# A spectral block and two MLPs on one core: bias written by ScalarE, another mixing unit in three float32r passes, two-bank tiles in the inverse transform

## The chip, the cores and the metric

The kernel runs on one core of one Trainium2 chip. The time is device microseconds of one execution; the median of the runs counts. Five engines work side by side: TensorE (PE: matmuls, and PEld: its weight loads), VectorE (DVE), ScalarE (ACT), GpSimd (POOL) and SyncE (SP). SyncE and GpSimd issue the transfers; an accumulating transfer (GpSimd's queue) adds its source to what lies at its destination.

## What is computed

Batch 2, 3008 positions, 256 channels. A real Fourier transform along the positions, a complex 256 x 256 mixing with a bias, a soft threshold on the real and the imaginary part, the inverse transform, then two MLPs (256 to 2048 to 256) over all 6016 tokens:

```python
X = np.fft.rfft(x, axis=1)
Yr = Xr @ w_r - Xi @ w_i + b_r
Yi = Xr @ w_i + Xi @ w_r + b_i
Yr = np.sign(Yr) * np.maximum(np.abs(Yr) - lam, 0.0)
...
y = np.fft.irfft(Y, n=x.shape[1], axis=1)
...
h = x @ w_in
g = h * (1.0 / (1.0 + np.exp(-1.702 * h)))
return (g @ w_out).astype(np.float32)
```

The second MLP has exp(-h) in place of exp(-1.702 h). Inputs and outputs are float32.

## The kernel before

**Stages.** Everything is unrolled, and within each engine the instructions keep the order in which the program writes them (`region(...)`, with a manual schedule). The stages are: the forward transform (16 groups, loop over `groups`), the mixing (12 units, loop over `mids`), the inverse (16 steps: q, b, t), and the MLPs (2 layers x 6 blocks of tokens x 8 parts, `group`). The forward and inverse transforms are matmuls against cosine and sine matrices, folded by symmetry.

**A mixing unit** (`mid_mm`) makes two groups of sums, each in one PSUM bank of 512 columns: a group is four matmuls of 512 columns. Units 0 and 1 (`n32` = 2) run them in float32, which the trace shows as two records per matmul. The later ones split both operands into a high and a low float32r part and make three passes (high x high, high x low, low x high). The first group also takes a matmul of ones against `bias_hl` (L572), whose row 0 is the high part of the bias, and row 1 the low part.

**Splitting.** `xsplit(i, 0)` makes the high part xh of unit i (a ScalarE copy, L500), `xsplit(i, 1)` the low part xl: ScalarE writes -x (L496), and a transfer on GpSimd's queue adds x (L497), so that the rounding is left. In the loop, iteration i makes xl of unit i + 3 and xh of unit i + 2; the first split unit's xl is made in forward group 10. The matrix's parts, wh (ScalarE, L550) and wl (VectorE, L551), are made at the stage's start.

**After a unit's matmuls**, one iteration later: ScalarE copies the first bank to SBUF (`us`, L578), VectorE makes sum and difference (`sd`, L580 to L582), ScalarE a relu (L588) and VectorE the threshold (L593); another iteration later VectorE folds (L605) into the inverse's operands. The threshold's two halves are separate instructions of 512 columns.

**Weight conversion beside it.** The MLP weights come as 64-bit floats and are converted on the way: load on SyncE (`raw`, L162 to L166), a ScalarE step (`cv_c`, L180), five VectorE steps (L185 to L189), and a transfer on GpSimd's queue that adds the rest (`cv_a`, L190). One is in work at a time. `tf` names the forward groups, `tm` the mixing units, `ti` the inverse steps in which one starts. The loads of the inverse's matrices (`load_m`, SyncE) stand in the units of `li` and the steps of `lii`.

**The inverse.** Two PSUM pools of four banks, ps0 and ps1. Steps with t = 0, 1 write two banks of ps0, steps with t = 2, 3 two banks of ps1 (`inv_mm`). One step later VectorE takes the banks out (`inv_post`): for t = 0, 1 into `rt`, after a ScalarE copy of one bank (`eo`, L697); for t = 2, 3 as `ac = rt + psi` and `rt = rt - psi` (L716, L717), bank by bank. `inv_out` writes the tokens into `yt`: two quarters by VectorE (L747), two by ScalarE (L749) and accumulating transfers (L751). `ac` is one SBUF tile, except for (q, b) = (1, 0). The last step's two halves are made inside the first MLP group. Step 8 of 16 is the ninth.

**The MLP** groups are matmuls without a gap in three passes each (L846, L874).

Of the kernel before, what the change touches and what calls it, by code (L numbers as in the profile page):

```python
# [9 lines left out]
F32 = mybir.dt.float32  # L10
CFG = {'lv0': 'V', 'lv': 'V', 'dd0': 'VPVVPPPPPVVP', 'dd': 'V', 'ths': 'VVVVPV', 'thf': 'V', 'ivf': 'V', 'cva': 'P', 'pol': 'PPPP', 'pil': 'P', 'mvl': 'PVVP', 'xl': 'V', 'xse': 'V', 'gl': 'VPPPPPPP', 'tf': [6, 10, 13], 'tm': [0, 2, 4, 6, 8, 10], 'ml': [], 'pk': 6, 'ti': [3], 'pi': 4, 'pl': [1, 4, 8, 10, 13], 'kb': [0, 1, 1, 1, 1, 1, 1, 0], 'kr': [0, 1, 0, 1, 0, 1, 1, 0], 'fa': 3, 'xp': [2, 4, 4, 5], 'xq': [1, 4, 1], 'xs': 4, 'xi': [7, 7, 9, 10, 10, 11, 8], 'xsi': 9, 'xo': (0, 1, 6, 2, 3, 4, 5), 'xd': (0, 1, 4, 6), 'ca': 4, 'tl': True, 'fwd': 'all', 'rest0': 'all', 'rest1': 'all', 'last1': 'all', 'inv': 'all', 'mid': 'all', 'last0': 'all', 'thm': 'A', 'gl0': 'PVPVVVPV', 'gl2': 'PPPPPPPP', 'gl3': 'PPPPPPPV', 'xl0': 'VVVVVPV', 'xl1': 'V', 'pre': 13, 'pre2': 0, 'yd': 6, 'lvb': 6, 'mlp': 'all', 'pr': 'V', 'pf': 'V', 'eo': '0111', 'n32': 2, 'li': [3, 5, 7], 'lii': [0], 'xa': 4, 'nhb': 6, 'ddb': 6, 'mlp1': 'all', 'mlp2': 'all'}
NUM = dict(li=[5, 6, 7, 8], n32=2, pk=4, ydp=2, lii=[1, 3], xd=(), ml=[], pl=[], xo=range(7), pi=6, nhb=6, tf=[5, 9, 13], tm=[1, 3, 5, 7, 9, 11], ti=[0, 2, 4, 6, 8, 10, 12, 14, 14, 15, 15], kb=[2] * 8, kr=1, fa=3, fe=2, pm=0, nf=4, lvb=6, ddb=8, ivb=1, eob=1, fsb=6, f1=3, f2=0, fm=[7, 8, 9], fi=[1, 1, 2, 2], pre=13, pre2=1, yd=3, psh=0, ie=[12], xp=[1, 3, 4, 5], xq=[1, 2, 2], xs=5, nw=4, xi=[14, 14, 15, 15], xsi=13, rw=2, ca=4, cc=2, tb=1, tmn=1)
# [9 lines left out]
P = 128  # L22
# [34 lines left out]
def spectral_mlp_kernel(ctx, tc, xin, mfwd, minv, wc, bias, w_in1, w_out1, w_in2, w_out2, outT):  # L57
# [4 lines left out]
    def N(k):  # L62
        return CFG.get(k, NUM[k])

# [486 lines left out]
    nc.vector.tensor_sub(wl, wc_s, r32(wh))  # L551

    def mid_mm(i):
        b, p, j = mids[i]
        x = [xt[b, p, j, cs][:, q] for cs in range(2) for q in range(2)]
        hl = [[xsp[b, p, j, cs, k][:, q] for k in range(2)] for cs in range(2) for q in range(2)] if i >= N('n32') else None
        ps = []
        for grp in range(2):
            t = bank(i, "psm")
            n = 0  # L560

            for xi, off in ((0, 0), (3, D)) if grp == 0 else ((1, 0), (2, D)):
                for mm in range(2):
                    w = slice(off, off + 2 * D)
                    if hl is None:
                        nc.tensor.matmul(t, x[xi][:, mm], wc_s[:, mm, w], start=(n == 0), stop=(n == 3 and grp == 1))  # L566
# [18 lines left out]
    def mid_relu(i, sd):  # L585
        th = mid_p.tile([P, 2, 512], F32, tag="th", name="th")
        for h in range(2):
            nc.scalar.activation(th[:, h], sd[:, h], AF.Relu, bias=neglam)  # L588
        return i, sd, th

    def mid_th(i, sd, th):
        for h in range(2):
            nc.vector.scalar_tensor_tensor(out=th[:, h], in0=sd[:, h], scalar=LAM, in1=th[:, h], op0=ALU.add, op1=ALU.min)  # L593
        return i, th

    def mid_fold(i, th):
        b, p, j = mids[i]
        for q in range(2):
# [14 lines left out]
            elif pairs:  # L613
                ft[q, b, p, -1] = ft.pop((q, b, p, 0))

    post = thr = None
# [31 lines left out]

    region('inv')
    modes[0] = True  # L650

# [4 lines left out]
    def inv_mm(q, b, t, mms=range(2), out=None):  # L656
# [21 lines left out]
    RW = 2 * 378  # L678

    def row(x, mm, t, n):  # L680
        if isinstance(x, dict):
            return x[t, mm][:, :n]
        return x[:, t * RW + mm * 378 : t * RW + mm * 378 + n]

    def inv_post(q, b, t, ps, mms=range(2)):
# [37 lines left out]
    def inv_out():  # L723
        q, b, ac, rt = ydone.pop(0)
        todo, col = [], b * S + (0 if q == 0 else HALF)
        for k in range(4):
            x = ac if k < 2 else rt
            if isinstance(x, dict):
                todo.extend((k, yt[:, mm, col : col + 376], x[0, mm][:, :376], x[1, mm][:, :376]) for mm in range(2))
                col += 376  # L730
                continue
            u, v = (x[:, t * RW : (t + 1) * RW].rearrange("p (m c) -> p m c", m=2) for t in range(2))
            if q == 0 and k == 1:
# [128 lines left out]
    def group(l, i, p, hook):  # L862
# [71 lines left out]
        if begun:  # L934
            out_next()
        else:
            inv_post(*prev[:3], inv_mm(*prev[:3], (1,), ps), (1,))
            inv_out()
        hook(5)
        prod(X, 2, 5, False)  # L940
# [236 lines left out]
```

## Time and profile before

| | |
|---|---|
| runs shown, median (lowest to highest) | 1147.75 us (1147.16 to 1149.87) |
| the profiled execution's own time | 1147.49 us |
| its span in the trace | 1145.7 us |
| TensorE busy | 1138.4 us (99%) |
| ScalarE, VectorE, GpSimd busy | 775.3, 609.0, 469.9 us |
| mixing stage | from 59.01 to 130.05 us |
| inverse, to the first matmul of the MLP | from 130.05 to 172.26 us |

The page gives the busy time of each engine, the costliest groups of instructions, and the chain of work that ended last. The stretch view gives busy time between two moments. The chain in order of time gives, for each piece, its start, its length and its engine, tile and line. The time views of one engine give start, length, line, form, and in brackets the idle time before it and what ended it. A record of a matmul is longer than its distance to the next, since matmuls overlap; lengths of the chain are distances.

### The profile page before, as it was taken

Reading aid. Unit: us, or ns where it says so; the run is one execution under the profiler, and the core shown is the slowest. Engines: PE = TensorE matmul, PEld = TensorE weight load, DVE = VectorE, ACT = ScalarE, POOL = GpSimd, SP = SyncE. Lnnn points to the kernel's source line nnn. Section 1 sums busy time; section 2 is a strip of 40 time slices with the busy share of each in tenths; the row PEclk is TensorE's granted clock in tenths of the full one; section 3 lists DMA queues with packets and bytes.
Section 4 is the critical chain, followed back from the end, with each engine's and each line's share of the span. In section 5 each row is a group of like instructions: output and inputs, shape, how many; then the busy total and the mean of one; then the engine's idle time right before and its main releaser. Section 6 shows DMA issues by size and latency. Waiting matters only on the chain.

```text
span 1145.7 us, 14644 instructions
## 1 busy us (share of the span) xinstructions
PE 1138.4 (99%) x5094; PEld 946.4 (83%) x5094; DVE 609.0 (53%) x1015; ACT 775.3 (68%) x1445; POOL 469.9 (41%) x410
## 2 busy tenths in 40 slices
PE   9999999999999999999999999999999999999998
PEld 6868987888888888888889878888888888888897
DVE  7888997764565465564554533523523523523422
ACT  2587357877677676686677876766765866756665
POOL 0253164444444434444446646443334433344333
PEclk9999999999999999999999999999999999999999
DMA  8699494431221212112211000010000100100100
GB/s 328 155 183 242 116 160 87 103 72 37 59 52 37 74 37 63 49 38 74 56 37 37 28 28 19 1 38 1 29 10 1 37 1 1 37 1 1 37 1 33
DMA packets 39852, 68.69 MB, mean 60 GB/s; under 512 B 3681, under 2 KB 16225, under 8 KB 39778
## 3 DMA queue, kind: packets, MB, share of 16 engines
q1 hardware_dynamic: 26306, 45.51, 12.2%
q0 software_dynamic: 13472, 22.24, 11.4%
q8 instruction: 40, 0.66, 0.2%
q14 instruction: 34, 0.28, 0.1%
HBM read 35.15 MB, written 10.35 MB: 40 GB/s over the span
## 4 chain that ended last, share of the span: by engine, by line
PE 95%; ACT 2%; DVE 2%; issue 1%; DMA 1%; SPq 0%; POOL 0%; DVEq 0%; POOLq 0%; ACTq 0%
PE o L846 43%; PE x L874 38%; PE psm L569 5%; PE psi L387 4%; PE psf L387 3%; PE psm L566 1%; ACT yt L877 1%; DMA xr<-in_x 1%; DVE keep L313 0%; SPq L477 0%; ACT g L879 0%; ACT yt L893 0%; PE psm L572 0%; ACT x L781 0%; DVE x L788 0%
## 5 line engine op out<-in xcount | busy, mean ns | idle before, releaser
L884 POOL TENSOR_TENSOR g<-yt,g 128x512 fp32r<-128x512 f32 (+1 forms) x282 | 357.6, 1282 | 502.8 <-PE x L874 316.7
L846 PE MATMUL o<-g,wo 128*128 128x512 f32 (+1 forms) x2304 | 559.8, 385 | 0.0
L846 PEld LDWEIGHTS o<-g,wo 128*128 128x128 f32 x2304 | 432.5, 188 | 80.8
L874 PE MATMUL x<-x,wi 128*128 128x512 f32 (+1 forms) x2016 | 498.5, 386 | 0.5
L874 PEld LDWEIGHTS x<-x,wi 128*128 128x128 f32 x2016 | 377.5, 188 | 75.1 <-ACT yt L893 1.7
L877 ACT ACTIVATE yt<-yt 128x512 f32<-128x512 f32 (+1 forms) x288 | 179.5, 623 | 263.6 <-DVE yt L924 216.6
L879 ACT CAST g<-yt 128x512 fp32r<-128x512 f32 (+1 forms) x384 | 236.0, 615 | 12.1
L924 DVE TENSOR_TENSOR yt<-yt,x 128x512 f32<-128x512 f32 (+1 forms) x96 | 64.8, 675 | 216.8 <-PE x L874 216.5
L896 DVE TENSOR_TENSOR yt<-yt,x 128x512 f32<-128x512 f32 (+1 forms) x96 | 64.9, 676 | 182.4 <-ACT yt L893 181.3
L884 DVE TENSOR_TENSOR g<-yt,g 128x512 fp32r<-128x512 f32 (+1 forms) x102 | 70.1, 687 | 65.9 <-ACT g L879 65.9
L190 POOL DMA_DIRECT2D cv_a<-cv_c x32 | 28.4, 889 | 111.4 <-DVE cv_c L189 105.0
L929 DVE TENSOR_TENSOR yt<-yt,x 128x512 f32<-128x512 f32 (+1 forms) x96 | 64.8, 675 | 0.3 <-issue 0.3
L788 DVE TENSOR_TENSOR x<-yt,x 128x512 fp32r<-128x512 f32 (+1 forms) x55 | 43.1, 783 | 36.1 <-ACT x L781 36.1
L877 ACT ACTIVATE yt<-x 128x512 f32<-128x512 f32 (+1 forms) x96 | 56.1, 584 | 0.0
L914 ACT COPY yt<-x 128x512 f32<-128x512 f32 (+1 forms) x96 | 55.8, 581 | 0.1
L912 ACT COPY yt<-x 128x512 f32<-128x512 f32 (+1 forms) x96 | 54.9, 572 | 1.4 <-PE x L874 1.4
L893 ACT COPY yt<-x 128x512 f32<-128x512 f32 (+1 forms) x96 | 54.9, 572 | 0.0
L387 PE MATMUL psi<-m,f 128*128 128x188 f32 (+3 forms) x224 | 45.2, 357 | 0.0
L387 PEld LDWEIGHTS psi<-m,f 128*128 128x128 f32 x224 | 37.6, 190 | 5.5
L387 PE MATMUL psf<-m,xf 128*128 128x190 f32 (+2 forms) x176 | 36.1, 366 | 0.6 <-DVE xf L332 0.6
L781 ACT CAST x<-yt 128x512 fp32r<-128x512 f32 (+1 forms) x59 | 36.5, 618 | 0.0
L387 PEld LDWEIGHTS psf<-m,xf 128*128 128x128 f32 x176 | 29.6, 190 | 7.3 <-DVE xf L332 0.9
(123 smaller groups left out, 803.9 us busy)
## 6 DMA issues: line engine op xcount, KB each, us to landing
raw<-in_wi SPq DMA_DIRECT2D x32, 256.0 KB, 3.6
cv_a<-cv_c POOLq DMA_DIRECT2D x32, 256.0 KB, 5.2
raw<-in_wo SPq DMA_DIRECT2D x16, 512.0 KB, 3.9
xl<-xt POOLq DMA_DIRECT2D x20, 256.0 KB, 8.4
out_t<-yt SPq DMA_DIRECT2D x20, 256.0 KB, 2.1
raw<-in_x SPq DMA_DIRECT2D x9, 512.0 KB, 6.3
wi<-tmp POOLq DMA_DIRECT2D x8, 256.0 KB, 4.8
w_in<-cv_a SPq DMA_DIRECT2D x8, 256.0 KB, 2.0
```

The lines of the kernel that those rows point to most:

```text
L387: nc.tensor.matmul(ps, hi[:, c : c + P], m[:, k, :w], start=i == 0, stop=i == last)
L569: nc.tensor.matmul(t, st, mv, start=n == 0 and k == 0, stop=n == 3 and grp == 1 and k == 2)
L846: nc.tensor.matmul(acc[h, mm], st, mv, start=first and k == 0, stop=last and k == 2)
L874: nc.tensor.matmul(ps, st, mv, start=first and m == 0, stop=m == 2, skip_group_check=True)
L877: nc.scalar.activation(g, g if src is None else src, func)
L879: nc.scalar.copy(gh, g)
L884: eng.tensor_sub(gl, g, r32(gh))
L893: nc.scalar.copy(y1, X)
L896: nc.vector.tensor_add(y1, y1, Y)
L914: nc.scalar.copy(y3, X)
L924: nc.vector.tensor_add(y2, y2, X)
L929: nc.vector.tensor_add(y3, y3, Z)
```

## The change

It does six things.

- The bias of units 4 to 11 is no longer a matmul: ScalarE copies it into the bank of the first group ahead of the unit (`put_bias(i + 1)` in iteration i, behind `mid_sd`), and the unit's matmuls add to what is there. The host gives the bias spread over 128 rows; it is loaded into `bias_f` in forward group 9.
- Unit 1 is split too (`n32` 2 to 1). Its xl is made in forward group 10; its xh and unit 2's xl at the stage's start.
- `tm` goes from [0, 2, 4, 6, 8, 10] to [1, 3, 5, 7, 9, 11].
- `li` goes from [3, 5, 7] to [6, 8, 9].
- Relu and threshold become one instruction of 1024 columns each.
- In the inverse ps1 is opened anew with two tiles of two banks, and steps with t = 2, 3 have both halves in one of them; VectorE takes both with one sum and one difference (the last step, inside the MLP, keeps its halves). `ac` of (0, 1) and (1, 0) lies in a part of `yt` that is written later. In the first MLP group ps1 is opened again with four banks.

```diff
-        nc.sync.dma_start(out=bias_f[0:1], in_=bias)
+        nc.sync.dma_start(out=bias_f[0:1], in_=bias[0:1])
...
+        if g == 9:
+            nc.sync.dma_start(out=bias_f, in_=bias)
         if g == 10:
-            xsplit(N('n32'), 1)
+            xsplit(1, 1)
...
+    xsplit(1, 0)
+    xsplit(2, 1)
...
-            t = bank(i, "psm")
+            ready = i in filled and grp == 0
+            t = filled.pop(i) if ready else bank(i, "psm")
...
-                            nc.tensor.matmul(t, st, mv, start=n == 0 and k == 0, stop=n == 3 and grp == 1 and k == 2)
+                            nc.tensor.matmul(t, st, mv, start=n == 0 and k == 0 and not ready, stop=n == 3 and k == 2 and (ready or grp == 1), skip_group_check=ready)
...
-            if grp == 0:
+            if grp == 0 and not ready:
                 nc.tensor.matmul(t, ones, bias_hl, start=False, stop=True)
...
-        for h in range(2):
-            nc.scalar.activation(th[:, h], sd[:, h], AF.Relu, bias=neglam)
+        nc.scalar.activation(th, sd, AF.Relu, bias=neglam)
...
-        for h in range(2):
-            nc.vector.scalar_tensor_tensor(out=th[:, h], in0=sd[:, h], scalar=LAM, in1=th[:, h], op0=ALU.add, op1=ALU.min)
+        nc.vector.scalar_tensor_tensor(out=th, in0=sd, scalar=LAM, in1=th, op0=ALU.add, op1=ALU.min)
...
+    def put_bias(i):
+        if 4 <= i < len(mids):
+            filled[i] = bank(i, "psm")
+            nc.scalar.copy(filled[i], bias_f)
...
         sd = mid_sd(*post) if post is not None else None
+        put_bias(i + 1)
         xsplit(i + 3, 1)
         xsplit(i + 2, 0)
...
+    closed("ps1")
+    ps_p[1] = opened("ps1", bufs=2, space=PS)
...
-        out = out or [bank(t // 2, "psi") for _ in range(2)]
+        if out is None and p:
+            d = ps_p[1].tile([P, 1024], F32, tag="pd", name="psi")
+            out = [d[:, :512], d[:, 512:], d]
+        out = out or [bank(0, "psi") for _ in range(2)]
...
-            if (q, b) == (1, 0):
-                ac[0] = {(h, mm): slot(1, F32, "ac") for h in range(2) for mm in range(2)}
+            if q != b:
+                ac[0] = [yt[:, :, c : c + 378 - 2 * q] for c in ((NT - 752, NT - 376) if q else (NT - 1504, NT - 1126))]
...
-        for mm in mms:
+        if len(mms) == 2:
+            r, a, d = both(rt[0], t - 2, n), both(ac[0], t - 2, n), ps[2].rearrange("p (m c) -> p m c", m=2)[:, :, :n]
+            nc.vector.tensor_add(a, r, d)
+            nc.vector.tensor_sub(r, r, d)
+        for mm in mms if len(mms) == 1 else ():
```

`both` gives the two halves of a tile as one operand. `mid_mm` in float32 (unit 0 alone now) is as it was.

## Rows read from the trace of the kernel before

**Rows 1.** The page, part 1: span; busy us (share) and instructions by engine.
```profile
span 1145.7 us, 14644 instructions
...
PE 1138.4 (99%) x5094; PEld 946.4 (83%) x5094; DVE 609.0 (53%) x1015; ACT 775.3 (68%) x1445; POOL 469.9 (41%) x410
```

**Rows 2.** Stretch view, TensorE: stretch, length, busy (instructions), clock, DMA share.
```profile
23.40:1142.20 1118.80, 1117.48 (x5018) 1.00 0.22 54
```

**Rows 3.** Chain by time: start us, length us, engine, tile, line, instructions.
```profile
59.01 3.43 PE psm L566 x8
...
62.67 6.87 PE psm L566 x16
...
87.57 5.45 PE psm L569 x24
93.02 0.23 PE psm L572
...
104.61 5.45 PE psm L569 x24
...
127.33 2.72 PE psm L569 x12
```

**Rows 4.** ScalarE by time, later in mixing: start, length, line [idle before].
```profile
101.53 0.57 ACT L578 COPY us<-psm 128x512 f32<-128x512 f32 x1
...
120.14 0.68 ACT L180 ACTIVATE cv_c<-raw 128x512 f32<-128x512 f32 x1 [2.01 <-DMA cv_a<-cv_c]
```

**Rows 5.** ScalarE by time, start of the mixing stage.
```profile
55.42 0.68 ACT L180 ACTIVATE cv_c<-raw 128x512 f32<-128x512 f32 x1 [3.54 <-DMA raw<-in_wi]
...
60.47 1.48 ACT L550 CAST wh<-wc_s 128x1536 fp32r<-128x1536 f32 x1
...
62.89 1.13 ACT L500 CAST xh<-xt 128x512 fp32r<-128x512 f32 x2
...
70.10 1.34 ACT L588 ACTIVATE th<-sd,neglam 128x512 f32<-128x512 f32 x2
```

**Rows 6.** VectorE by time, start of the mixing stage.
```profile
61.98 1.76 DVE L551 TENSOR_TENSOR wl<-wc_s,wh 128x1536 fp32r<-128x1536 f32 x1
```

**Rows 7.** Tile view of xl, its last line.
```profile
DMA to landing us min/median/max: 3.5/8.4/10.8
```

**Rows 8.** DMA issues, 60 to 66 us: queue, KB each, median landing us.
```profile
xl<-xt POOLq DMA_DIRECT2D x2, 256.0 KB, 3.9
```

**Rows 9.** DMA issues, 40 to 135 us.
```profile
xl<-xt POOLq DMA_DIRECT2D x20, 256.0 KB, 8.4
...
m<-in_mi SPq DMA_DIRECT2D x2, 384.0 KB, 9.7
...
m<-in_mf SPq DMA_DIRECT2D x1, 376.0 KB, 3.6
bias_hl<-bias_f POOLq DMA_DIRECT2D x1, 2.0 KB, 2.7
```

**Rows 10.** POOL's queue by time, end of the forward stage.
```profile
43.62 0.54 POOL L367 DMA_DIRECT2D bias_hl<-bias_f  x1 [4.71 <-DVE bias_f L366]
```

**Rows 11.** SyncE's queue by time, end of the forward stage.
```profile
49.03 0.38 SPq L162 DMA_DIRECT2D raw<-in_wi  x1
```

**Rows 12.** VectorE by time, end of the mixing stage and inverse.
```profile
121.67 0.43 DVE L185 TENSOR_SCALAR cv_c<-cv_c 128x512 f32<-128x512 f32 x1
...
123.79 0.69 DVE L189 SCALAR_TENSOR_TENSOR cv_c<-raw,cv_c 128x512 f32<-128x512 uint32 x1
...
130.16 0.69 DVE L580 TENSOR_TENSOR sd<-us,psm 128x512 f32<-128x512 f32 x1 [0.81 <-PE psm L569]
...
149.26 0.55 DVE L429 TENSOR_TENSOR rt<-psi,eo 128x376 f32<-128x376 f32 x1
```

**Rows 13.** Stretch view of psi, inverse to its ninth step.
```profile
130.05:150.70 20.65, 20.65 (x129) 20.65 (x129) 7.40 (x14) 1.91 (x4) 1.00 0.45 94
```

**Rows 14.** Tile view of yt, 150 to 165 us: min/median/max ns, forms.
```profile
L747 DVE TENSOR_TENSOR yt<-rt x3: 544/549/947, 156.9 to 158.2; 128x752 f32<-128x752 f32 x1, 128x376 f32<-128x376 f32 x1, 128x374 f32<-128x374 f32 x1
```

More of the change, by code (lines that the diff above doesn't have):

```diff
@@ L10 @@
 F32 = mybir.dt.float32
-CFG = {'lv0': 'V', 'lv': 'V', 'dd0': 'VPVVPPPPPVVP', 'dd': 'V', 'ths': 'VVVVPV', 'thf': 'V', 'ivf': 'V', 'cva': 'P', 'pol': 'PPPP', 'pil': 'P', 'mvl': 'PVVP', 'xl': 'V', 'xse': 'V', 'gl': 'VPPPPPPP', 'tf': [6, 10, 13], 'tm': [0, 2, 4, 6, 8, 10], 'ml': [], 'pk': 6, 'ti': [3], 'pi': 4, 'pl': [1, 4, 8, 10, 13], 'kb': [0, 1, 1, 1, 1, 1, 1, 0], 'kr': [0, 1, 0, 1, 0, 1, 1, 0], 'fa': 3, 'xp': [2, 4, 4, 5], 'xq': [1, 4, 1], 'xs': 4, 'xi': [7, 7, 9, 10, 10, 11, 8], 'xsi': 9, 'xo': (0, 1, 6, 2, 3, 4, 5), 'xd': (0, 1, 4, 6), 'ca': 4, 'tl': True, 'fwd': 'all', 'rest0': 'all', 'rest1': 'all', 'last1': 'all', 'inv': 'all', 'mid': 'all', 'last0': 'all', 'thm': 'A', 'gl0': 'PVPVVVPV', 'gl2': 'PPPPPPPP', 'gl3': 'PPPPPPPV', 'xl0': 'VVVVVPV', 'xl1': 'V', 'pre': 13, 'pre2': 0, 'yd': 6, 'lvb': 6, 'mlp': 'all', 'pr': 'V', 'pf': 'V', 'eo': '0111', 'n32': 2, 'li': [3, 5, 7], 'lii': [0], 'xa': 4, 'nhb': 6, 'ddb': 6, 'mlp1': 'all', 'mlp2': 'all'}
+CFG = {'lv0': 'V', 'lv': 'V', 'dd0': 'VPVVPPPPPVVP', 'dd': 'V', 'ths': 'VVVVPV', 'thf': 'V', 'ivf': 'V', 'cva': 'P', 'pol': 'PPPP', 'pil': 'P', 'mvl': 'PVVP', 'xl': 'V', 'xse': 'V', 'gl': 'VPPPPPPP', 'tf': [6, 10, 13], 'tm': [1, 3, 5, 7, 9, 11], 'ml': [], 'pk': 6, 'ti': [3], 'pi': 4, 'pl': [1, 4, 8, 10, 13], 'kb': [0, 1, 1, 1, 1, 1, 1, 0], 'kr': [0, 1, 0, 1, 0, 1, 1, 0], 'fa': 3, 'xp': [2, 4, 4, 5], 'xq': [1, 4, 1], 'xs': 4, 'xi': [7, 7, 9, 10, 10, 11, 8], 'xsi': 9, 'xo': (0, 1, 6, 2, 3, 4, 5), 'xd': (0, 1, 4, 6), 'ca': 4, 'tl': True, 'fwd': 'all', 'rest0': 'all', 'rest1': 'all', 'last1': 'all', 'inv': 'all', 'mid': 'all', 'last0': 'all', 'thm': 'A', 'gl0': 'PVPVVVPV', 'gl2': 'PPPPPPPP', 'gl3': 'PPPPPPPV', 'xl0': 'VVVVVPV', 'xl1': 'V', 'pre': 13, 'pre2': 0, 'yd': 6, 'lvb': 6, 'mlp': 'all', 'pr': 'V', 'pf': 'V', 'eo': '0111', 'n32': 1, 'li': [6, 8, 9], 'lii': [0], 'xa': 4, 'nhb': 6, 'ddb': 6, 'mlp1': 'all', 'mlp2': 'all'}
 NUM = dict(li=[5, 6, 7, 8], n32=2, pk=4, ydp=2, lii=[1, 3], xd=(), ml=[], pl=[], xo=range(7), pi=6, nhb=6, tf=[5, 9, 13], tm=[1, 3, 5, 7, 9, 11], ti=[0, 2, 4, 6, 8, 10, 12, 14, 14, 15, 15], kb=[2] * 8, kr=1, fa=3, fe=2, pm=0, nf=4, lvb=6, ddb=8, ivb=1, eob=1, fsb=6, f1=3, f2=0, fm=[7, 8, 9], fi=[1, 1, 2, 2], pre=13, pre2=1, yd=3, psh=0, ie=[12], xp=[1, 3, 4, 5], xq=[1, 2, 2], xs=5, nw=4, xi=[14, 14, 15, 15], xsi=13, rw=2, ca=4, cc=2, tb=1, tmn=1)
@@ L565, in mid_mm @@
                     if hl is None:
-                        nc.tensor.matmul(t, x[xi][:, mm], wc_s[:, mm, w], start=(n == 0), stop=(n == 3 and grp == 1))
+                        nc.tensor.matmul(t, x[xi][:, mm], wc_s[:, mm, w], start=n == 0, stop=n == 3 and grp == 1)
                     else:
                         for k, (st, mv) in enumerate(passes(hl[xi][0][:, mm], hl[xi][1][:, mm], wh[:, mm, w], wl[:, mm, w])):
-                            nc.tensor.matmul(t, st, mv, start=n == 0 and k == 0, stop=n == 3 and grp == 1 and k == 2)
+                            nc.tensor.matmul(t, st, mv, start=n == 0 and k == 0 and not ready, stop=n == 3 and k == 2 and (ready or grp == 1), skip_group_check=ready)
                     n += 1
-            if grp == 0:
+            if grp == 0 and not ready:
                 nc.tensor.matmul(t, ones, bias_hl, start=False, stop=True)
@@ L614, in mid_fold @@
                 ft[q, b, p, -1] = ft.pop((q, b, p, 0))
+    filled = {}
+    def put_bias(i):
+        if 4 <= i < len(mids):
+            filled[i] = bank(i, "psm")
+            nc.scalar.copy(filled[i], bias_f)
     post = thr = None
@@ L678, in spectral_mlp_kernel, with both @@
     RW = 2 * 378
+    def both(x, t, n):
+        if isinstance(x, list):
+            return x[t][:, :, :n]
+        return x[:, t * RW : (t + 1) * RW].rearrange("p (m c) -> p m c", m=2)[:, :, :n]
     def row(x, mm, t, n):
-        if isinstance(x, dict):
-            return x[t, mm][:, :n]
+        if isinstance(x, list):
+            return x[t][:, mm, :n]
         return x[:, t * RW + mm * 378 : t * RW + mm * 378 + n]
@@ L727, in inv_out @@
             x = ac if k < 2 else rt
[L728 to L732, printed above, removed]
+            u, v = x if isinstance(x, list) else (x[:, t * RW : (t + 1) * RW].rearrange("p (m c) -> p m c", m=2) for t in range(2))
             if q == 0 and k == 1:
@@ L938, in group @@
             inv_out()
+            closed("ps1")
+            ps_p[1] = opened("ps1", bufs=4, space=PS)
         hook(5)
@@ L1160 @@
         "in_wc": wc,
-        "in_bias": np.concatenate([inputs["b_r"], inputs["b_i"]])[None],
+        "in_bias": np.ascontiguousarray(np.broadcast_to(np.concatenate([inputs["b_r"], inputs["b_i"]]), (P, 2 * D))),
         "in_wi1": np.ascontiguousarray(inputs["moe_w_in"]).view(np.int64),
```

## The prediction

> **What bounds the kernel now.** I read the page's busy times first, then the stretch view of TensorE, then the chain in order of time through the mixing stage, and only then the other engines there. The page: TensorE is busy for 1138.4 of 1145.7 us, no other engine over 68% [rows 1]. The stretch view narrows it: from 23.40 to 1142.20 us TensorE lacks 1.32 us of being busy, at a granted clock of 1.00 [rows 2]. So in the changed stages the chain is a row of matmuls, and what is taken from them moves the end, unless another engine or a transfer that now hides behind them comes out. Only 1.32 us of waits are left to win.
>
> The chain gives the prices [rows 3]. A mixing unit of plain float32 is 16 TensorE records, 6.87 us. A unit in three float32r passes is 24 records, 5.45 us. The bias matmul is 0.23 us more in each of the 12 units. A three-pass unit with its bias lasts 5.68 us.
>
> **The sum on TensorE.** Unit 1 goes from 16 float32 records to 24 float32r ones: 6.87 - 5.45 = 1.42 us. Units 4 to 11 lose their bias matmul: 8 x 0.23 = 1.84 us. Nothing is added to TensorE: the inverse keeps its products and only writes them into one tile of two banks. Together 3.26 us.
>
> The new unit has the form of ten units already timed, 5.45 / 24 = 0.227 us a matmul [rows 3]. The Trainium skill, page "TensorE: Matmul & The Clock Gate", section "Back-to-back issue gap", states some 131 ns per matmul of 512 columns in a stream of weight loads and matmuls; by that the two terms would be 3.73 and 1.05 us. The trace disagrees, and I go by the row.
>
> **What is added elsewhere, and its cover.**
> - ScalarE fills a bank with the bias, 8 times. The nearest rows are the 512-column copy out of PSUM, 0.57 us [rows 4], and a cast of a pair of 512-column tiles, 1.13 us [rows 5]: 0.57 us each, 4.6 us in all. The fill for unit i+1 stands right behind the us copy of unit i-1. At the latest such place I looked at, us of unit 6 ends at 102.10, the fill would end near 102.7, and unit 8 starts at 107.33 (half of the 24 records from 104.61) [rows 3, 4]. The 4.6 us between hide it. Behind the fill on ScalarE stand the unit's xl and xh, two or three units ahead of their use.
> - Unit 1's xh and unit 2's xl are made at the stage's start. xh(1) follows wh, which ends at 61.95, and costs 1.13 us [rows 5]: 63.1. wl ends at 63.74 [rows 6]. Unit 1 starts at 66.1 (middle of the 16 records from 62.67) [rows 3], so there are 2.4 us to spare; its xl comes from the forward stage, as unit 2's does now. xl(2) leaves ScalarE near 64.2; its two accumulating transfers are issued on POOL near 64 and 65. Unit 2 starts at 66.1 + 5.68 = 71.8 and wants the first low half two matmuls later, 72.25, the other at 73.6. A transfer lands after 3.5 to 10.8 us, 8.4 at the median [rows 7], and the two of 60 to 66 us took 3.9 [rows 8]. I take 3.9: it is the same queue at the same time, and the conversion of unit 0, with its transfers on POOL's queue, is moved behind it; unit 1 adds two such transfers to twenty. So 69 us, no wait; the other ends are 0 and a wait of 2.5 us or so.
> - The 256 KB bias load on SyncE waits until the bias's low row has been copied: 43.62 + 2.7 = 46.3 us [rows 9, 10]. Behind it in the queue is the weight load of 49.03 [rows 11], which stands later anyway. Scaled from 376 KB in 3.6 us [rows 9] the transfer takes 2.5 us, in a busy stretch. ScalarE already waits 3.54 us for that weight load at 55.42 [rows 5], so 1 us of delay goes to wh, wl and xh(1), inside the 2.4 us.
> - Conversions in odd units: their instructions, five on VectorE, one on POOL, the weight load on SyncE, are the same six times. Matrices at 6, 8 and 9: the slowest took 9.7 us to land [rows 9]; the first is behind unit 5's weight load, near 97 us, and is wanted at 126.8; the third is wanted 20 us into the inverse. Nothing.
> - One relu and one threshold on 1024 columns for two on 512: below the 1.34 us of the ScalarE pair [rows 5], above one of them. Off the path; what it costs is that relu starts after the whole of sd.
>
> **The inverse is where cover is thin.** VectorE runs without a pause to speak of from 130.16, and frees step 4's banks at 149.26 + 0.55 = 149.81 [rows 12]; the ninth step, which takes them, starts at 150.70 [rows 13]. 0.89 us to spare. In the changed kernel the mixing stage ends at 127.33 + 2.72 - 3.26 = 126.79 and the ninth step starts at 147.44. But the last conversion, 2.8 us of VectorE [rows 12], now lies in unit 11 and not 10. From unit 10's end (121.34) VectorE has unit 10's sums (1.3, two 0.69 us of work overlapping a little), a fold (1.3), the conversion (2.8) and a threshold (1.2) before unit 11's sums: 127.9. From there to the freed banks it took 19.65 us before; minus 0.1 for the threshold, and minus 4 x 0.14, since a two-bank sum of 752 columns is 0.95 us [rows 14] and two of 376 are 1.10: 19.0. So 146.9, 0.5 us to spare instead of 0.89, and no wait. Its bounds: no wait, and, with the whole conversion late by its own length, 2.8 - 0.5 = 2.3 us. I take none, because the count above leaves a margin and every term in it is a duration of this stage. The ac sums of two of the four (q, b) now lie in yt, so the wait of one batch's sums for the other's transfer goes; it is VectorE's and small.
>
> The sum goes against the profiled execution's own 1147.49 us: 1147.49 - 3.26 = 1144.23. The median of the runs shown, 1147.75, is 0.26 above, so the forecast is 1144.5 us, 0.28% down. A measurement of this kernel can tell about 0.3% from no change, 3.44 us: the forecast lies just inside it.
>
> **The rivals.**
> - VectorE late in the inverse. The last conversion waits for its predecessor's transfer: ScalarE's start of it waited 2.01 us at 120.14, 1.4 us into unit 10 [rows 4]. If the spacing of the conversions doesn't shrink with the units (10.9 us a pair, not 11.36), it slips by 0.46 us a pair, up to 2.3 us over five, and TensorE waits for banks in steps 4 to 10. Past 0.5 us of slip it costs one for one; with a two-bank tile freed only as a whole, up to 2.3 us: 1145.0 to 1146.8. For it: rows 12, 13. Against: the matrix loads leave the early units, which speeds the transfers. Chance 0.15.
> - The other side: the bias load. If it holds up the weight load by more than 2.4 us, ScalarE, which stops at 55.42 for it, is late with wh and TensorE waits in unit 1; xl(2), late by the same and landing at the usual 8.4 us, adds 2.5 us in unit 2. From about 3.2 us of delay this is over 3.26 us. At 5 us, between the 2.5 us above and the 9.7 us of the slowest row, 5.1 us are lost: 1149.6, and 1148 to 1152 around it. Against it: in the same stretch two transfers of 256 KB landed in 3.9 us [rows 8], so that much delay takes several of them in the way. Chance 0.04.
> - The change doesn't take the bias off the path: the first matmul of each seeded bank waits for ScalarE by as much as it saved. 1144.5 + 1.84 = 1146.3. Against it: 4.6 us of distance. Chance 0.06.
> - More is won: some of the 1.32 us of waits [rows 2] goes too, as VectorE is freer in the inverse. 1143.2 to 1144.2. Chance 0.10.
> - Closer matmuls in unit 1 and in the others: at the 0.131 us of the page above the time would be 1143.0; ten units at 0.227 us speak against it. Chance 0.01.
>
> **How the numbers follow.** The forecast, 1144.5, keeps 0.64; its own range is 1143.8 to 1145.3. The bound for "faster" is 1144.31, for "slower" 1151.19. Of the forecast's case 0.45 lies below 1144.31, that is 0.29; with 0.10 and 0.01 faster is 0.40. Slower is half of the bias load's case, 0.02. The rest, 0.58, is no change. The range takes in the forecast's own, most of the gain of waits, the late VectorE and the seeded bank: 1143.2 to 1146.9.
>
> **What would show it.** Right: unit 1 as 24 records in 5.45 us; units 4 to 11 following each other every 5.45 us with no L572 in the chain; the first psi matmul near 126.8 us; the stretch view with about the same 1.3 us unbusy. Wrong: a stall ahead of unit 1 or 2 that ends on xh, wl or xl; psm matmuls waiting for the ScalarE copy of the bias; psi matmuls in steps 4 to 10 waiting for VectorE's rt or ac; conversions' starts slipping against the units.

## The result and the profile after

The changed kernel takes 1155.24 us (median, 1154.96 to 1156.22), against 1148.47 us for the kernel before on the same chip: 1.0065, 95% interval 1.0052 to 1.0077. It is 0.65% slower, outside the range and on the side that had a chance of 0.02. The profiled execution took 1155.07 us, its span is 1153.3 us.

The page's busy times against [rows 1]: TensorE is busy for as long, in a longer span.

```profile
span 1153.3 us, 14622 instructions
...
PE 1139.0 (99%) x5094; PEld 948.9 (82%) x5094; DVE 606.6 (53%) x989; ACT 777.2 (67%) x1443; POOL 470.7 (41%) x410
```

The chain by time through the start of the mixing stage, against [rows 3]:

```profile
58.75 3.43 PE psm L572 x8
62.18 0.23 PE psm L578
62.41 3.43 PE psm L572 x8
65.84 2.77 PE psm L575 x12
```

After the 16 float32 records of unit 0, the first group of unit 1 is 12 records in 2.77 us (0.23 apart), so the unit is in three passes. The mixing did what was forecast. Next, four stretches of the stretch view: the mixing of the kernel before and of the changed one, from the first psm matmul to the first psi matmul, then for the same two the 56 us that follow. The columns after the length: busy us (instructions) of TensorE, its weight loads, VectorE, ScalarE, POOL; granted clock, DMA share, GB/s.

```profile
59.01:129.89 70.88, 70.88 (x285) 53.21 (x284) 63.27 (x128) 49.42 (x88) 25.39 (x29) 1.00 0.94 199
...
129.89:185.89 56.00, 56.00 (x284) 47.79 (x283) 49.04 (x94) 33.30 (x61) 26.63 (x26) 1.00 0.68 122
```

```profile
58.75:126.29 67.54, 67.54 (x285) 53.19 (x285) 59.66 (x113) 51.31 (x88) 26.68 (x31) 1.00 0.99 203
...
126.29:182.29 56.00, 48.44 (x239) 41.40 (x237) 42.90 (x72) 26.54 (x46) 22.67 (x22) 0.94 0.69 131
```

The mixing lasts 67.54 us instead of 70.88, 3.34 us less; the forecast was 3.26. Then it is lost: in the first 56 us of the inverse TensorE gets 239 records done instead of 284, and from the first psi matmul to the end of the span it is 1153.3 - 126.29 = 1027.0 us instead of 1145.7 - 129.89 = 1015.8, so 11.2 us more. The same rows show why in part. VectorE was idle 70.88 - 63.27 = 7.6 us of the mixing before and 67.54 - 59.66 = 7.9 us after: its idle time didn't shrink with the stage, and up to 3.6 us of its work go over into the inverse. The DMA share rose from 0.94 to 0.99 of 16 engines.

What TensorE waits for in the inverse (the waits from 126 to 186 us: us in all, times, longest), where the kernel before was busy throughout:

```profile
PE psi L387 <- ACT eo L719: 5.2, 1, 5.2
PE psi L387 <- DVE rt L429: 1.2, 2, 0.9
PE psi L387 <- DVE rt L739: 0.7, 2, 0.4
```

Two causes, then: ScalarE once, for 5.2 us, and VectorE several times. ScalarE by time, the rows that answer to [rows 4] and those around the long wait:

```profile
69.12 0.66 ACT L180 ACTIVATE cv_c<-raw 128x512 f32<-128x512 f32 x1
...
126.81 0.67 ACT L180 ACTIVATE cv_c<-raw 128x512 f32<-128x512 f32 x1 [3.67 <-DMA cv_a<-cv_c]
...
156.23 0.82 ACT L771 ACTIVATE yt<-yt 128x754 f32<-128x754 f32 x1
164.73 0.82 ACT L771 COPY yt<-yt 128x752 f32<-128x752 f32 x1 [7.68 <-DMA yt<-yt]
...
167.53 0.46 ACT L719 COPY eo<-psi 128x376 f32<-128x376 f32 x1
```

The second quarter of tokens of (0, 1) is copied only at 164.73, after 7.68 us of waiting for a transfer; behind it in ScalarE's order stands the eo copy, which would free a bank of TensorE's. The transfer waited for is the first quarter's, in the chain by time:

```profile
157.34 7.30 DMA yt<-yt
```

It runs from 157.34 to 164.64, and the copy starts 0.09 us later. This is the mixing's first conversion in the kernel before; 69.12 is that of the changed one:

```profile
65.10 0.68 ACT L180 ACTIVATE cv_c<-raw 128x512 f32<-128x512 f32 x1 [1.08 <-DMA raw<-in_wi]
```

From it to the last, at 120.14 [rows 4], are five steps of 11.0 us on average; from 69.12 to 126.81 in the changed kernel five of 11.5, though two units take 10.9 us there instead of 11.36. In the changed kernel each of these five starts waits for the transfer `cv_a` of the conversion before it (0.35 to 3.67 us), and this transfer lands after 7.1 us at the median of 60 to 130 us, where it took 5.6. VectorE by time, against [rows 12]:

```profile
116.28 0.43 DVE L185 TENSOR_SCALAR cv_c<-cv_c 128x512 f32<-128x512 f32 x1 [1.30 <-ACT cv_c L180]
...
123.85 0.68 DVE L586 TENSOR_TENSOR sd<-us,psm 128x512 f32<-128x512 f32 x1
...
127.51 0.43 DVE L185 TENSOR_SCALAR cv_c<-cv_c 128x512 f32<-128x512 f32 x1 [1.12 <-ACT cv_c L180]
...
137.75 0.55 DVE L727 TENSOR_TENSOR rt<-psi,eo 128x380 f32<-128x380 f32 x1
...
168.02 0.55 DVE L723 TENSOR_TENSOR rt<-psi,eo 128x376 f32<-128x376 f32 x1 [9.41 <-ACT eo L719]
```

Its first sum of the inverse comes at 137.75. In the kernel before, the same sum is this:

```profile
136.61 0.55 DVE L705 TENSOR_TENSOR rt<-psi,eo 128x380 f32<-128x380 f32 x1
```

So TensorE enters the inverse 3.6 us earlier than before, and VectorE 1.1 us later.

### The profile page after: what moved, and what is told of

Same layout as the page of the kernel before. It is cut to its first block, busy times and chain, and to the rows that moved or that the text cites. A ratio compares the mean times of both kernels' runs of the same rounds, so it can differ in the third digit from the quotient of the medians.

```text
span 1153.3 us, 14622 instructions
## 1 busy us (share of the span) xinstructions
PE 1139.0 (99%) x5094; PEld 948.9 (82%) x5094; DVE 606.6 (53%) x989; ACT 777.2 (67%) x1443; POOL 470.7 (41%) x410
## 4 chain that ended last, share of the span: by engine, by line
PE 86%; issue 5%; ACT 3%; DMA 2%; DVE 2%; POOL 2%; SPq 0%; POOLq 0%; DVEq 0%; ACTq 0%
PE o L868 43%; PE x L896 38%; PE psf L387 3%; DMA xl<-xt 1%; PE psi L387 1%; POOL xl L497 1%; DMA yt<-yt 1%; ACT yt L899 1%; PE psm L572 1%; DMA xr<-in_x 1%; PE psm L575 0%; DVE keep L313 0%; DMA raw<-in_x 0%; POOL wi L106 0%; POOL cv_a L190 0%
## 5 line engine op out<-in xcount | busy, mean ns | idle before, releaser
L387 PE MATMUL psi<-m,f 128*128 128x188 f32 (+3 forms) x224 | 49.0, 372 | 7.6 <-ACT eo L719 5.2
```

Of the source, the lines that this page charges most:

```text
L387: nc.tensor.matmul(ps, hi[:, c : c + P], m[:, k, :w], start=i == 0, stop=i == last)
```

## The experiments

Theory after the trace: (A) `ac` of (0, 1) in yt makes the ScalarE copy wait, and the eo copy with it; (B) the rest is lost because the conversions, paced by transfers, did not come earlier with the units, so that VectorE is late. Rivals: the two-bank tiles hold TensorE; ScalarE's fills hold it.

### ac in the output tile

**Its own tile** for (0, 1), the rest as changed:

```diff
-            if q != b:
+            if (q, b) == (1, 0):
                 ac[0] = [yt...
```

> The changed kernel, with the ac of (q, b) = (0, 1) in its SBUF tile as before; only (1, 0) keeps it in yt. Theory: ScalarE's copy of the second quarter of (0, 1) waited 7.68 us for the transfer of the first, because both name yt as source and destination; TensorE then stood still for 5.4 us and ran some 6.8 us at half clock. With ac out of yt the wait goes, and with it 5.4 us and about 2.2 us of half clock: 1147.6 us, within 0.7 us; granted clock 1.00 throughout. Rival, that the transfer queue itself is late there (its landing took 7.3 us): the wait stays as a wait of the same copy or of the ac sums, and the time stays over 1152 us.

1148.10 us, ratio 1.0003 (0.9992 to 1.0013): no 7.68 us wait, clock 1.00 throughout. Some 6.8 of the 11.2 us go (1020.2 us from the first psi matmul on, 4.4 more than before): some 7 us of the loss are A, the rest stays. Of these 4.4 us the waits view shows 2.7 as TensorE's waits for VectorE's `rt`, the longest 1.4 us in step 4. The next four runs leave `ac` in yt and change how it is read.

**Both copies ahead of the transfers**, `ac` in yt:

```diff
             (nc.scalar.mul(y, v, -1.0) if k == 0 else nc.scalar.copy(y, v))
+        for k, y, u, v in todo:
+            if k > 1:
+                continue
             for yy, uu in ...
```

> The changed kernel, with ac in yt, but in each batch of outputs both ScalarE copies are issued ahead of the accumulating transfers. Theory of the wait through yt: the second copy no longer has a transfer ahead of it to wait for, so 1147.6 us as in the run with ac in its tile, within 0.7 us of it. Rival, the late transfer queue: no gain, over 1152 us.

1154.14 us (1.0058): a miss. The copy starts at 159.01, but now the second quarter's transfers wait for the first's to land, and the sum of (1, 0), whose `ac` is in yt too, waits for them.

**The copy in two halves**, each a three-dimensional operand instead of one of four dimensions with gaps:

```diff
...
+            elif (q, b) == (0, 1):
+                for g in range(2):
+                    nc.scalar.copy(y[:, :, g], v[:, :, g])
```

> The changed kernel, with the second quarter's ScalarE copy of (0, 1) made as two copies of one half each, so that its operand has three dimensions instead of four; nothing else moved. If the wait comes from the four-dimensional operand with gaps (its two halves are 188 columns at a distance of 189), no copy waits, and the time is 1147.6 us and some 0.3 us for a copy more. If any copy within yt waits for a transfer out of yt, the first of the two waits as before and the time stays near 1155 us. For the first: the same copy of (1, 0), with three dimensions, did not wait.

1154.47 us (1.0057): right on the copies, a miss on the time. ScalarE by time:

```profile
160.15 0.90 ACT L775 COPY yt<-yt 128x376 f32<-128x376 f32 x2
```

POOL's queue by time, and VectorE:

```profile
160.54 1.36 POOL L779 DMA_DIRECT2D yt<-yt  x1
168.60 2.41 POOL L779 DMA_DIRECT2D yt<-yt  x2 [6.70 <-DVE rt L429]
```

```profile
173.52 0.94 DVE L738 TENSOR_TENSOR yt<-rt,psi 128x752 f32<-128x752 f32 x1 [4.04 <-DMA yt<-yt]
```

The two short copies wait for nothing, though they write and read the same columns as the one that had waited 7.68 us. The transfers of the second quarter, still whole, now wait in its place, and VectorE for them. So:

**Copy and transfers both in halves**:

```diff
...
+            if (q, k, b) == (0, 1, 1):
+                pieces = [(y[:, :, g], u[:, :, g]) for g in range(2)]
...
```

> The changed kernel with ac in yt; the second quarter of (0, 1) is copied and transferred half by half (188 columns of both channel halves each), so that neither its ScalarE copies nor its transfers have the operand of four dimensions, or the pair of pieces with a gap. With the copy alone split, no copy waited, but the second quarter's transfers still stood 6.70 us behind the landing of the first. Theory that the wait belongs to the shape with the gap: the transfers follow each other, and the time is that of the run with ac in its tile, 1148.1 us, within 1 us. Rival, that any transfer from yt to yt waits for the one ahead: the second stands some 7 us behind the first, and the time stays over 1152 us.

1148.74 us (1.0003, 0.9994 to 1.0012), with `ac` in yt. POOL's queue by time:

```profile
159.09 3.80 POOL L783 DMA_DIRECT2D yt<-yt  x3
```

All three transfers go out at once. The same columns in the same tile, and no wait: it hangs on the shape of the operand, not on the data. How the wait is derived from the shape is not shown by any row.

**Matrix loads at 3, 5, 7** on top of the second run (`'li': [6, 8, 9]` to `[3, 5, 7]`):

> The run with both copies first, and the inverse's matrices loaded in units 3, 5 and 7 again. On top of the stall of 5.4 us the changed kernel has stalls of 2.7 us in steps 3 to 8 of the inverse, since VectorE ends the mixing late: the last conversion waited 3.67 us for its predecessor's transfer, which took 7.4 us beside a matrix load, 5.4 us before. Theory that the matrix load beside it does this: the transfer takes 5.4 us again, the conversion starts 2 us earlier, and the stalls shrink to 0.7 us: 1145.6 us. Rival, that the odd units alone put the conversion too late: 1147.6 us, no difference from the run with both copies first.

1153.93 us (1.0061): a miss. The transfers' wait of the second run covers everything else, so the time says nothing on theory B; the trace does. The last conversion's L180 waits 1.32 us and starts at 125.31, where it waited 3.63 us and started at 127.09 in the second run, and TensorE's idle time ahead of step 4 falls from 1.34 to 0.60 us.

### The fills and the conversions' units

Conversions back in the even units, `ac` in its own tile; then with the matrix loads at 3, 5, 7 as well; then with the whole inverse of before as well:

```diff
-'tm': [1, 3, 5, 7, 9, 11]
+'tm': [0, 2, 4, 6, 8, 10]
```

> The run with ac of (0, 1) in its tile, and the conversions in units 0, 2, ... 10 again; matrices stay at units 6, 8 and 9. That run's TensorE stalls of 3.6 us in steps 4 to 10 of the inverse are put down to the last conversion, in unit 11: it delays VectorE's first sums of the inverse to 137.8 us and later. Theory: with the last conversion in unit 10 VectorE comes 3 us or more earlier, the stalls fall under 0.5 us, and the time is 1147.05 - 3.0 = 1144.1 us, within 0.6 us. Rival, that the two-bank tiles, freed only as a whole, are what holds TensorE: stalls of 2 us or more stay, and the time is over 1146 us. A second rival: the conversion in unit 0 holds up the high and low parts of units 1 and 2, with a stall before 75 us.

> The run before with the matrices at units 3, 5 and 7 as well: the mixing's numbers as before the change, the other parts as changed. Both theories expect the time of the run before within 0.5 us, since nothing waits for a matrix; if the matrices at units 3 to 7 lengthen the transfers there beyond a unit's reach, stalls of the mixing matmuls show it, 0.5 to 2 us.

> The kernel before with the change's mixing stage alone: bias by ScalarE, unit 1 in three float32r passes, relu and threshold in one instruction. Conversions in even units, matrices at 3, 5 and 7, and the inverse with single banks and ac as before. The sum on TensorE is 3.26 us and the mixing stage of the changed kernel had no stall: 1147.05 - 3.26 = 1143.8 us, within 0.6 us. If the inverse's two-bank tiles are worth something, this is slower than the two runs before, with VectorE late in steps 4 to 10; if they cost, it is faster.

1151.44, 1151.29 and 1151.30 us (1.0030, 1.0022, 1.0023): misses by 7 us. In the first, the waits of TensorE's weight loads from 76 to 96 us (TensorE itself stands 4.1 us), and ScalarE by time:

```profile
PEld psm L575 <- ACT psm L625: 4.5, 1, 4.5
```

```profile
82.19 0.67 ACT L180 ACTIVATE cv_c<-raw 128x512 f32<-128x512 f32 x1 [5.90 <-DMA raw<-in_wi]
86.12 0.59 ACT L625 COPY psm<-bias_f 128x512 f32<-128x512 f32 x1
```

ScalarE stands 5.90 us at a conversion whose weights haven't landed, and the fill of unit 4's bank (L625) stands behind it in its order. The weight loads wait for the same line in the other two, 3.0 and 1.9 us. It is near the prediction's rival of the seeded bank, but with one long wait at unit 4 instead of a short one at each bank; it is absent in the changed kernel, whose longest wait in the mixing is 0.2 us. In the third profile (an execution of 1149.41 us) TensorE itself stands 1.1 us for it, and 2.4 us for VectorE in the inverse, so this wait is only a part of the miss there. With the fill two units ahead (`put_bias(i + 2)`), the same three kernels, the second and third with loads at 3, 5, 7:

> The changed kernel with (0,1)'s ac in its SBUF tile, the conversions back in the even units, and each unit's bias copied into its bank two units ahead instead of one. Theory 1 (what cost 4.2 us in the same kernel with the fill one unit ahead is that the copy of unit 4's bias stood behind a conversion that ScalarE could not start, and nothing else): no stop of TensorE over 1 us ahead of units 4 to 11, no half clock there, the last conversion's first pass 3 us earlier than with odd units, and a median near 1146 (1151.4 less 4.2 and some 1.3 of half clock), 0.999 of the kernel before. Rival (the banks themselves come free too late when ScalarE is held, since its evacuations stand behind the conversion as well): TensorE still stops 2 us or more near 85 us, and the median is 1149 or more.

> As the run above, and the matrix loads at units 3, 5 and 7 as in the kernel before. Theory 1: no stop near 85 us, the step-4 stop of the inverse at most 0.6 us, a median near 1145.7. Rival (evacuations held too): 1149 or more. Third possibility (loads at 3, 5, 7 hold the conversions' transfers up): the conversions' first passes come later than in the run above and the median is above it by 1 us or more.

> The kernel before (its inverse, conversions in even units, matrix loads at 3, 5, 7) with the mixing's two changes alone: bias by ScalarE, now two units ahead, and unit 1 in three passes. Theory 1 (the fill one unit ahead cost 1.3 us and the clock after it, and what was gained in the mixing is partly lost again to VectorE in the inverse): no stop near 84 us, some 3 us of stops in steps 4 to 14 of the inverse as with the fill one ahead, a median near 1148 (1151.3 less 1.3 and some 1.5). Rival (the whole gain of the mixing shows once no fill is late): 1144.5, 0.997 of the kernel before.

1150.19, 1150.85 and 1150.80 us (1.0017, 1.0021, 1.0024): misses by 3 to 5 us. The wait on L625 is gone, and another has its place; the weight loads from 76 to 126 us in the third:

```profile
PEld psm L575 <- DMA xl<-xt: 2.6, 1, 2.6
```

The low parts xl, too, are begun by ScalarE behind the conversion, which waits 5.53 us for its weights here (5.57 in the first); the transfers of these parts are issued from 87.44 us on and land late as well, after 8.9 us at the median of 80 to 100 us. Moving the fill moved the stop from unit 4 to a later unit: ScalarE is held as before, and what stands next behind it is late in its place. In the inverse TensorE waits another 2.7 to 3.5 us for VectorE in these three.

### Where the rest of the gain goes

From here on: conversions in odd units, the fill one unit ahead, and, but for the two runs with the inverse of before, `ac` in its own tile. **Four of the five VectorE passes of the last conversion left out** (2.0 us of VectorE's work; that half matrix is not converted):

> The changed kernel with (0,1)'s ac in its SBUF tile, and four of the five VectorE passes of the last conversion of the mixing (unit 11) left out: that half matrix is wrong by it, and VectorE has 2.0 us less to do just ahead of the inverse. Theory 1 (VectorE comes late into the inverse because its work between 60 and 140 us is as much as before while the mixing is 3.3 us shorter): the stop in step 4 of the inverse falls from 1.6 us to about 0, those of steps 6 to 10 (0.6, 0.5, 0.5) shrink or go, and the median is 1145.5 to 1146.5 (1148.1 less about 2). Rival (the stops come from the two-bank tiles, which hold both banks until both sums of a pair are done): the stops stay within 0.3 us and the median is 1148.1.

1147.29 us (0.9995, 0.9986 to 1.0004). The stop in step 4 fell from 1.6 to 0.3 us (from start to start of the matmuls; as idle time, 1.41 to 0.18), those of steps 6 to 10 stayed: 0.8 us won at the median where 2 were expected, and the intervals of this run and of the first overlap. VectorE's work is what step 4 waits for.

**Seven folds by POOL** (`'thf'`, P at the odd folds of units 4 to 10):

> The changed kernel with (0,1)'s ac in its SBUF tile, and the odd folds (q = 1) of units 4 to 10 by POOL instead of VectorE: seven operations of 128x512, 0.6 us each on VectorE, 1.28 us each on POOL by the same shape elsewhere. Theory 1 (VectorE's work is what the inverse waits for): VectorE reaches the inverse's first sum some 3 to 4 us earlier, the stops in steps 4 to 10 go, and the median is about 1144.8, 0.998 of the kernel before. Rival a (two-bank tiles hold TensorE): 1148.1. Rival b (POOL's folds hold up the transfers that it issues for the conversions and splits, or slow VectorE beside them): the conversions' first passes come later still, or TensorE stops in the mixing, and the median is over 1148.1.

1150.33 us (1.0020): the time of rival b. The last L180 came at 129.33 instead of 127.75, but 1.0 of these 1.6 us was there at the stage's second conversion (83.92 against 82.91), ahead of the first fold by POOL. And VectorE was not relieved: two of its folds, at 100.42 and 112.55, ran beside folds of POOL and took 2.58 and 2.52 us, the others 0.7 to 0.8. POOL by time, the second of the two:

```profile
112.22 2.29 POOL L609 TENSOR_TENSOR f<-th 128x512 f32<-128x512 f32 x1
```

VectorE is busy for 59.53 us of the mixing, with all folds on VectorE 59.41, so this run is no test of theory 1.

**Unit 1 in plain float32** again (`'n32': 2` and its first splits as before):

> The changed kernel with (0,1)'s ac in its SBUF tile, and mixing unit 1 in the four-pass form of the kernel before (1.4 us longer on TensorE by the trace, two splits less on ScalarE and POOL). Theory 1 (VectorE and the conversions' transfers set when the inverse can go on): the mixing ends 1.4 us later, the stops in the inverse are 1.4 us shorter in sum, and the median is 1148.1 within 0.5. Rival (TensorE's time counts wherever it is saved): 1149.5, the stops unchanged.

1147.38 us (0.9996, 0.9987 to 1.0005): nothing is lost by giving up a gain of 1.42 us, though the interval overlaps that of the run with three passes (0.9992 to 1.0013). Then the same with **matrix loads at 3, 5, 7**, and beside it the three-pass unit with those loads, and this with the one-bank inverse of before:

> The changed kernel with (0,1)'s ac in its SBUF tile, unit 1 in the four-pass form, and the matrix loads at units 3, 5 and 7 as before (conversions stay in odd units). Theory (the load at unit 9 makes the last conversion's transfer some 2 us longer, and this comes out in the inverse): the last conversion's first pass comes 1.5 to 2.5 us earlier (126.8 without it), the stops in the inverse fall from 2.1 us to about 1.2 (steps 8 and 10 stay, if they are the two-bank tiles'), the median is about 1146.4, 0.999 of the kernel before. Rival (the transfer's length doesn't depend on that load): 1147.4.

> The same with unit 1 in three passes: the changed kernel with (0,1)'s ac in its SBUF tile and the matrix loads at 3, 5 and 7. Theory: the step-4 stop falls from 1.6 to 0.8 us (as the matrix load did with ac in the output tile), median 1147.2. Rival (loads without effect): 1148.1.

> The changed kernel's mixing (bias by ScalarE, unit 1 in three passes, conversions in odd units) with the matrix loads at 3, 5 and 7 and the whole inverse of the kernel before, one-bank tiles. If the two-bank tiles cost what steps 6 to 10 show (1.6 us in sum): no stops there, a median 1145.6 to 1146.2. If one-bank tiles stop TensorE as much where VectorE is late (1.7 us at step 8 with conversions in even units): 1147 to 1148.5.

1146.91 us (0.9991, 0.9982 to 0.9999), 1149.79 us (1.0009) and 1149.00 us (1.0007), on the same chip. The first is 0.5 us above its forecast, with the last L180 2.5 us earlier, as expected; the other two are misses, by 2.6 and by at least 0.5 us. Unit 1 in three passes **costs** 2.9 us here. The third has one-bank tiles, and TensorE waits 3.8 us for `rt` in its inverse, against 3.5 us in the second: so these waits do not come from the two-bank tiles. The stretch view of the first two, the mixing and the 56 us after it; the columns are as above. The profiled executions took 1146.03 us, the fastest of 11, and 1151.65 us, the slowest of 12, so these two views lie 5.6 us apart and show the difference larger than the medians have it:

```profile
58.68:127.80 69.12, 69.12 (x279) 51.89 (x277) 63.53 (x121) 53.48 (x91) 26.20 (x30) 1.00 0.91 191
...
127.80:183.80 56.00, 55.67 (x280) 46.97 (x279) 50.07 (x82) 32.40 (x57) 26.36 (x25) 1.00 0.76 140
```

```profile
58.91:128.73 69.82, 68.41 (x286) 53.04 (x285) 58.89 (x111) 52.57 (x91) 27.93 (x32) 1.00 0.94 197
...
128.73:184.73 56.00, 52.12 (x260) 43.12 (x259) 51.26 (x85) 30.64 (x53) 23.82 (x23) 1.00 0.76 140
```

VectorE gets 63.53 us done in the mixing with unit 1 in float32, and 58.89 with it in three passes; TensorE's first 56 us of the inverse are then nearly full (280 records) or have 3.9 us of stops (260). Why, by POOL's queue in time and then ScalarE in time, of the float32 version:

```profile
65.48 1.75 POOL L497 DMA_DIRECT2D xl<-xt  x2 [2.67 <-DMA raw<-in_wi]
68.04 1.75 POOL L497 DMA_DIRECT2D xl<-xt  x2 [0.81 <-ACT xl L496]
```

```profile
80.37 0.66 ACT L180 ACTIVATE cv_c<-raw 128x512 f32<-128x512 f32 x1
...
124.34 0.67 ACT L180 ACTIVATE cv_c<-raw 128x512 f32<-128x512 f32 x1 [1.47 <-DMA cv_a<-cv_c]
```

the last line of its view of tile raw, 55 to 100 us:

```profile
DMA to landing us min/median/max: 3.3/3.8/7.3
```

and the same three of the three-pass version:

```profile
66.16 5.36 POOL L497 DMA_DIRECT2D xl<-xt  x6 [3.71 <-ACT xl L496]
```

```profile
85.14 0.66 ACT L180 ACTIVATE cv_c<-raw 128x512 f32<-128x512 f32 x1 [3.95 <-DMA raw<-in_wi]
...
129.21 0.69 ACT L180 ACTIVATE cv_c<-raw 128x512 f32<-128x512 f32 x1 [1.21 <-DMA cv_a<-cv_c]
```

```profile
DMA to landing us min/median/max: 3.2/7.1/10.1
```

The split of one more unit puts six xl transfers of 256 KB back to back at the stage's start. The weight loads of the conversions, on another queue, then land after 7.1 us at the median of this stretch instead of 3.8, the second conversion of the stage starts at 85.14 instead of 80.37, and the chain of conversions never catches up: 129.21 instead of 124.34 for the last. Held by them, ScalarE is late with fills as well: the weight loads wait 2.4 us for L625 in this mixing, TensorE itself 1.4.

The other traces with conversions in odd units bear out the start of this chain. The weight loads of 70 to 82 us land after 7.2 to 8.6 us at the median in the seven with unit 1 in three passes, and after 4.7 to 4.9 in the three with float32; the second conversion starts at 81.67 to 85.14, and at 80.03 to 80.47. The last conversion depends on the matrix loads as well: with float32 and loads at 6, 8, 9 it starts at 126.82, as late as in the changed kernel, but the mixing ends 1.6 us later there, at 127.90. No run takes the two transfers away alone: the split also gives ScalarE two more pairs of operations, and the share of each isn't separated.

**The bias by ScalarE alone** (the float32 version above with the inverse of before):

> Of the change, the bias by ScalarE alone, with the conversions in odd units: unit 1 in four passes, matrix loads at 3, 5 and 7, the inverse with one-bank tiles as before. If the two-bank tiles only matter where VectorE is late: 1146.9 within 0.5, as the run with them. If they save something: 1147.5 or more, with stops at steps 4 and 8 of the inverse. If they cost: 1146.3 or less.

1147.26 us (0.9996, 0.9987 to 1.0005), 54.78 us of TensorE in the 56 us after the mixing against 55.67 with two-bank tiles. Whether these are worth the 0.35 us between the two medians stays open. Against this run, unit 1 in three passes costs 1.7 us with one-bank tiles (1149.00 us above).

The best version, 1146.91 us, has the bias by ScalarE, conversions in odd units, relu and threshold in one, two-bank tiles, `ac` of (0, 1) in its own tile, and leaves unit 1 in float32 and the matrix loads where they were. It is faster than the changed kernel by 0.7% and than the kernel before by 0.09%, whose interval just excludes 1. It is the lowest of 18 kernels timed, and the intervals of the three next to it (0.9995 to 0.9996) include 1, so a gain over the kernel before is not shown.

From the first psi matmul on, in the profiled executions, whose own times stand beside the medians (us):

| kernel | first psi | from there to the span's end | profiled | median | ratio |
|---|---|---|---|---|---|
| before | 129.89 | 1015.8 | 1147.49 | 1147.75 | 1 |
| changed | 126.29 | 1027.0 | 1155.07 | 1155.24 | 1.0065 |
| ac in its tile | 126.67 | 1020.2 | 1148.68 | 1148.10 | 1.0003 |
| and unit 1 in float32 | 127.90 | 1018.2 | 1147.89 | 1147.38 | 0.9996 |
| and loads at 3, 5, 7 | 127.80 | 1016.4 | 1146.03 | 1146.91 | 0.9991 |
| unit 1 in three passes, loads at 3, 5, 7 | 128.73 | 1021.2 | 1151.65 | 1149.79 | 1.0009 |

## Why the prediction was wrong

- **The sum on TensorE was right**: 3.26 us forecast, 3.34 measured, unit 1's matmuls 0.23 us apart. The 131 ns of the Trainium skill ("TensorE: Matmul & The Clock Gate", "Back-to-back issue gap") would put that group of 12 at 1.6 us, an estimate; it took 2.77.
- **The bias load** did no harm: TensorE's longest wait in the mixing is 0.2 us.
- **The fills' cover** ("the 4.6 us between hide it") held in the changed kernel, but not with conversions in even units. It was taken at one place in a trace with conversions in even units, where ScalarE waited 2 us; with the fill in place and the same units ScalarE stood 5.90 us and TensorE 4.1.
- **"Conversions in odd units ... Nothing" and the 0.5 us to spare** failed. The count let VectorE begin unit 10's sums at 121.34 and go on to the conversion at 121.34 + 2.6 = 123.9. It began the sums at 123.85, since the conversion before had made it late (116.28, after 1.30 us of waiting for its L180), and the conversion at 127.51, after 1.12 us more: that L180 had waited 3.67 us for the transfer before it. The rival had this mechanism, priced up to 2.3 us with a chance of 0.15; what stays of the loss without A is 4.4 us (1020.2 against 1015.8), more than the gain, and 2.7 of it are TensorE's waits for VectorE. The evidence was in the trace: a DMA share of 0.94 over the whole mixing, a row I had not asked for. The conversions hang on transfers, and their spacing didn't shrink with TensorE's work: 11.5 us from one to the next, before 11.0. My argument against the rival, that the matrix loads leave the early units, left out where they go: with the loads back at 3, 5, 7 the last conversion starts earlier in two pairs of traces (127.09 to 125.31, 126.82 to 124.34), if not in a third (127.75 to 129.21). The two xl transfers that I counted as "two such transfers to twenty" fell into a full stretch. The Trainium skill ("DMA: Bandwidth & Descriptors", "Issuing engines are not separate DMA queues") says that transfers started by different engines run on the same 16 DMA engines and interleave. The landing of raw, 7.1 us against 3.8, agrees.
- **"The wait of one batch's sums for the other's transfer goes; it is VectorE's and small"** was the dearest step. I looked at the wait that goes, and not at what now reads and writes the same tile: the copy waited 7.68 us, behind it eo, behind that TensorE. No rival had it. It is some 7 of the 11.2 us.
- **The other side** was forecast through the bias load alone, 0.02 for slower; it came by two other mechanisms, each of which gives back more than the gain.

## What to carry to other kernels

Before pricing work that is taken from the busiest engine of a stage, read the stage's DMA share and what the other engines' chains wait for. Where the transfers are nearly full (here 0.94 of 16 engines before, 0.99 after) and a chain of loads, steps and transfers runs beside the engine, time won there can be given back at the next point where the two meet. Before moving a temporary into an output tile, list every instruction and transfer on that tile and the shapes of their operands, and what stands behind each in its engine's order. An engine that keeps its order and may be held by a transfer is a bad place for a step that TensorE waits for, unless the hold is in another part of the cycle.

## What was not expected of the hardware

TensorE's stop in the inverse cost more than its own length. The stretch view of the changed kernel around it, in steps of 2 us:

```profile
164.00:166.00 2.00, 0.00 (x0) 0.00 (x0) 0.00 (x0) 1.27 (x3) 0.16 (x1) 0.94 0.01 2
166.00:168.00 2.00, 0.00 (x0) 0.00 (x0) 0.00 (x0) 1.99 (x5) 2.00 (x4) 0.50 0.22 30
...
170.00:172.00 2.00, 2.00 (x8) 2.00 (x8) 1.97 (x4) 0.89 (x3) 0.08 (x1) 0.50 1.08 180
172.00:174.00 2.00, 2.00 (x12) 2.00 (x11) 1.97 (x5) 2.00 (x5) 0.00 (x0) 0.85 0.56 94
```

While TensorE stood, the granted clock fell from 1.00 to 0.50 (from 2.4 to 1.2 GHz), and it stayed there after TensorE had resumed at 168.04, until some time in the stretch from 172 us. At the lower clock it does 8 records of 128x188 in 2 us; with `ac` in its own tile, at 1.00, it does 14 to 15 of the same step. The 32 records of this form take 7.6 us here and 5.3 there, so the lower clock adds 2.3 us to the stop of 5.2.

Shorter stops had the same effect in other traces. The clock fell to 0.50 after TensorE had stood 4.1, 2.6 and 2.2 us in the mixing (first two runs with conversions in even units, third with the fill two units ahead) and after 2.0 us in the run with copy and transfers in halves. After 2.0 us it stayed at 1.00 in two others (the copy in halves; unit 1 in three passes with loads at 3, 5, 7), and with `ac` in its own tile, where TensorE stands 1.4 us at most, it stays at 1.00.
